# Two-level gates of two blocks from the fifth group on, with attention's turns copied by ScalarE and the leftovers' norm in three parts

## The chip, the cores and the metric

The kernel runs on one core of a Trainium2 chip. Its time is the device time of one execution, in microseconds (us). A profile of one execution is read beside it. The engines are named as the profile names them: PE (TensorE, with PEld for its weight loads), DVE (VectorE), ACT (ScalarE), POOL (GpSimd) and SP (SyncE, which here only issues DMAs).

## What is computed

An attention block without softmax is followed by a multiplicative feed-forward block. All arithmetic is in float32.

```python
# q, k, v: (8 batches, 8 heads, 576 tokens, 64)
kv  = einsum('bhsd,bhse->bhde', k, v)
o   = einsum('bhsd,bhde->bhse', q, kv)
x   = o / sqrt(mean(o*o, axis=-1, keepdims=True) + 1e-06) * g_norm
x   = x.transpose(0, 2, 1, 3).reshape(8 * 576, 512)
out = ((x @ w1) * (x @ w2)) @ w3 @ w_out   # w1, w2: 512x1024; w3: 1024x1024; w_out: 1024x512
```

## The kernel before

**Groups.** The 4608 tokens are worked on in nine groups of 512: groups 0 to 6 are the first 512 tokens of batches 0 to 6, then comes group 8, the 64 leftover tokens of all eight batches, and group 7 (batch 7) is last. The kernel counts them by T in the order 0, 1, ..., 6, 8, 7. w3 @ w_out is folded into one matrix (w3o) at the start. A group has two parts: the *gates*, which make a = x @ w1, b = x @ w2 and their product, and the *projection* of the product with w3o.

**One-level gates.** The 1024 columns of the gates are cut into four pairs of blocks, p = 0 to 3. `gates(T, p, ...)` computes one pair by Winograd's form of Strassen's scheme (`winograd`): seven products instead of eight, each of two weight matrices by two chunks of 128, so 28 matmuls of 128x128 weights by 256 moving columns. Sums of weights (s1 to s4) are kept in SBUF; sums of the inputs (t1 to t4) are made once a group by `combine_x`, in the projection before. After a product ScalarE copies it out of PSUM (`keep`), because the next product is added on top of it in the same bank, or VectorE adds two and multiplies the a half by the b half (`multiply`: L784, L785).

**Two-level gates.** For the last two groups, T = 8 and 7 (`TWICE`), blocks p = 0 and 1 are done together with the scheme applied twice (`gates_of_two`): seven products for each of the two weight matrices (w), each of seven matmuls of 128x128 by 128 columns, 98 in all. The second-level sums of the weights are made by `prepare_w` in seven steps during groups 3 and 4, stored in DRAM (`w_l2`), and loaded as three parts into the three buffers called `streams`, which the projection uses too. `replace_a21` overwrites the weights' a21 quarters with the fourth sum, in group 6. The second-level sums of the inputs are 28 subtractions of 128x128 on GpSimd (`sum_x`, L844 to L847). ScalarE copies accumulators (L888, L889), VectorE adds others to them in halves (`add`, L893 and L894), and `finish` makes four quarters of the result from seven places of an accumulator (L905 to L908), with the gate product (L910) for the second w. The order of such a group is: gates of p = 2, two-level gates of p = 0 and 1, gates of p = 3, projection. The projection (`project_twice`) is two-level in every group from 1 on; its first matmuls read the gate product c11 of the block p = 3 and the inner sums made from it (`sum_inner`).

**Attention for the next group.** `steps(b)` hands out pieces of the attention of batch b, where b = T + 1. `between()` runs one piece at two places of each one-level block, eight a group:

- `begin_kv`: PE's kv products (L339) of two pairs of heads, copied by ScalarE (L350).
- `finish(h)`: PE's products q by kv (L415) of half h, and `norm`: ScalarE squares (L383), VectorE sums (L384), ScalarE takes the root (L388), VectorE inverts (L390) and multiplies into `xn` (L393).
- `q_two_by_dma`, `x_by_dma`: a transpose of 512 columns through DMA. Before it, GpSimd copies the tile into two planes of 16 bits (L296, L298); SP issues the transpose (L300); after it, GpSimd copies the planes back together (L310). `turn(i, ...)` begins one in piece i and ends it one piece later.
- In odd batches, `product_left` (L434) with its norm, for the leftover queries of two batches, and `x_left_by_dma`.

**Order.** PE, GpSimd and SP run in the order in which the code is written. VectorE does so from block p = 3 to the end of a projection, and in `gates_of_two`; elsewhere VectorE and ScalarE are ordered by a scheduler, with `tc.issue_after(x)` placing an instruction behind x on its engine. PSUM has eight banks: five in the pool `ps_mm` (gates and projection), three in `ps_at` (attention, and the accumulator r3 of the two-level gates).

Of the kernel before, what the change touches and what calls it, by code (L numbers as in the profile page):

```python
# [22 lines left out]
def kernel(  # L23
# [40 lines left out]
    KF = DF // P  # L64
    NH = KF // 2
# [254 lines left out]
    def attention(b):  # L320
# [41 lines left out]
        def q_by_dma(r):  # L362

            qT[r] = work.tile([P, 2, 2, P], FP32, name="qT")
            q_sb = loaded["q", b, r].rearrange("p e n -> p (e n)")
            to = qT[r].rearrange("p e i t -> p (e i t)")
            return turn_by_dma([q_sb], to, q_sb, [to], q_copy)
# [3 lines left out]
        def q_left_by_dma():  # L371
# [3 lines left out]
            return turn_by_dma([src], to, src, [to], q_copy)  # L375

        def norm(o_ps, dsts):

            n, w = len(o_ps), o_ps[0].shape[1]
            inv = work.tile([P, n, w // D], FP32, name="inv")  # L380
            for i in range(n):
                sq = work.tile([P, G], FP32, name="sq")[:, 0:w]
                nc.scalar.activation(sq, o_ps[i], AF.Square)  # L383
                nc.vector.tensor_reduce(  # L384
                    out=inv[:, i], in_=sq.rearrange("p (h d) -> p h d", d=D), axis=AX.X, op=ALU.add
# [39 lines left out]
        def product_left():  # L425
# [16 lines left out]
            all_of(norm(o_ps, [xn[:, :, e:e + 1, :] for e in range(2)]))  # L442
# [10 lines left out]
        def x_by_dma(h, copy=nc.gpsimd.tensor_copy):  # L453
# [4 lines left out]
            half = [slice(r * G, (r + 1) * G) for r in range(2)]  # L458
            return together(
                turn_by_dma(  # L460
                    [xn[:, :, r * P:(r + 1) * P]], flat[:, half[r]], turned[:, half[r]], [x[:, :, r]],
                    copy,
                )
                for r in range(2)
            )

# [37 lines left out]
        def finish(h):  # L504
# [4 lines left out]
            q_two_by_dma, q_left_by_dma, x_by_dma, x_left_by_dma,  # L509
        )})  # L510

    batches = {}

    def batch(b):
        if b not in batches:
            batches[b] = attention(b)
        return batches[b]

    def steps(b):
# [25 lines left out]
        odd = b % 2  # L545
        if b == 1:
# [12 lines left out]
        if b == 1:  # L559
# [19 lines left out]
            ends[5].append((end, "left", "u3"))  # L579
        else:  # L580
# [8 lines left out]
        if odd:  # L589
            fs[second].append((a.product_left,))  # L590
# [3 lines left out]
        else:  # L594
            turn(5, a.x_by_dma, 1)
            if odd:
                turn(5, a.x_left_by_dma, next_group=more)
        if more:
            turn(7 if b == 1 else 5, batch(b + 1).q_two_by_dma, 0, 1, next_group=True)
# [39 lines left out]
    def winograd(lhsT, rhs, chunks, done, between=lambda: None, keep_u3=True):  # L639
# [17 lines left out]
        def keep(name, ps):  # L657
            t = late_tile(name)[:, 0:4, :].rearrange("p (u a) n -> p u (a n)", u=2)
            copies.setdefault(name, []).append(nc.scalar.copy(t, ps))  # L659
            late[name] = t  # L660
# [109 lines left out]
    def gates(T, p, between, ready=lambda name: None):  # L770
# [4 lines left out]
        def multiply(name, one, two):  # L775

            dst = ab[int(name[1]) - 1][:, p, int(name[2]) - 1, :]
            if two is None:
                c = late_pool.tile([P, N], FP32, name="c21")
                nc.scalar.copy(c, one[:, 0, :])  # L780
# [15 lines left out]

    def prepare_w():
# [631 lines left out]
```

## Time and profile before

| what | us |
|---|---|
| median of 3 runs | 759.11 (758.6 to 759.81) |
| the profiled execution | 758.72 |
| its span, first to last instruction | 756.9 |
| PE busy in the span | 749.4 |
| DVE busy | 589.4 |
| ACT busy | 267.0 |
| POOL busy | 164.1 |
| group T = 5 (467.08 to 542.52 of the span) | 75.44 |
| group T = 8 (617.26 to 685.20) | 67.94 |

The granted clock of TensorE is 1.00 throughout. A profile line of a group of instructions gives line, engine, operation, the tiles as out<-in, shapes, how many, then busy time and the mean of one in ns, then how long the engine had been idle before them and what ended that. In the chain of waits each line gives start, length, and what ran; weight loads are counted together with matmuls there.

### The profile page before, as it was taken

To read this page: it belongs to the slowest core of one execution; us is meant where nothing else is said; L and a number is where in the kernel's file an instruction comes from. 1 tells how busy PE (TensorE), PEld (TensorE's weight loads), DVE (VectorE), ACT (ScalarE), POOL (GpSimd) and SP (SyncE) were. 2 spreads that over 40 slices of the span, in tenths; PEclk is the share of its full clock that TensorE was granted. 3 is DMA by queue.
4 is the path that set the end of the run, shared out by engine and by line. 5 is a ranking of instruction groups with operands and counts; after the bars stand their busy time and mean duration, and the time that the engine had idled before them with its cause. 6 is when DMAs were issued, how large, how long until landed. Compare 5 with 4: busy or idle time off the path is not lost.

```text
span 756.9 us, 14948 instructions
## 1 busy us (share of the span) xinstructions
PE 749.4 (99%) x5903; PEld 657.7 (87%) x5903; DVE 589.4 (78%) x1171; ACT 267.0 (35%) x492; POOL 164.1 (22%) x190
## 2 busy tenths in 40 slices
PE   8999999999999999999999999999999999999998
PEld 5455788888899889988998899889988999999997
DVE  7977999639888568758975897567776778996897
ACT  6777787312322232223222322232223223222321
POOL 0000000322511441144114410431143124006000
PEclk9999999999999999999999999999999999999999
DMA  9996954349997845675767567745743470465244
GB/s 319 344 334 177 273 163 102 85 104 271 336 299 248 225 114 177 223 205 141 218 218 210 155 192 223 208 103 173 224 125 53 150 225 28 146 211 186 87 152 139
DMA packets 146554, 143.20 MB, mean 189 GB/s; under 512 B 86580, under 2 KB 133812, under 8 KB 146484
## 3 DMA queue, kind: packets, MB, share of 16 engines
q1 hardware_dynamic: 144032, 127.82, 58.1%
q10 hardware_dynamic: 2452, 14.42, 5.7%
q8 instruction: 47, 0.77, 0.4%
q14 instruction: 23, 0.19, 0.1%
HBM read 105.78 MB, written 19.14 MB: 165 GB/s over the span
## 4 chain that ended last, share of the span: by engine, by line
PE 97%; DVE 1%; DMA 1%; ACT 1%; issue 0%; SPq 0%; ACTq 0%
PE mm L646 55%; PE mm L1075 23%; PE mm L625 7%; PE mm L875 5%; PE at L339 3%; PE at L415 2%; PE at L612 1%; PE at L875 1%; DMA raw<-in_moe_w_out_dram 1%; PE at L1126 0%; DVE ab L163 0%; PE at L358 0%; PE at L434 0%; DVE chunks L170 0%; SPq L198 0%
## 5 line engine op out<-in xcount | busy, mean ns | idle before, releaser
L646 PE MATMUL mm<-xT,w_sb 128*128 128x256 f32 x720 | 165.2, 380 | 0.0
L646 PEld LDWEIGHTS mm<-xT,w_sb 128*128 128x128 f32 x720 | 136.6, 191 | 18.3 <-issue 0.5
L646 PE MATMUL mm<-xc,ws 128*128 128x256 f32 x512 | 116.2, 380 | 0.0
L646 PEld LDWEIGHTS mm<-xc,ws 128*128 128x128 f32 x512 | 97.3, 190 | 13.7 <-ACT p L659 0.8
L296 POOL COPY xT<-xn 128x1024 uint16<-128x1024 uint16 x26 | 31.2, 1227 | 171.9 <-DVE xn L393 171.9
L784 DVE TENSOR_TENSOR c<-mm,u 128x512 f32<-128x512 f32 x32 | 22.0, 689 | 58.4 <-PE mm L646 58.4
L659 ACT COPY u<-mm 128x512 f32<-128x512 f32 x58 | 34.0, 585 | 93.4 <-PE mm L646 82.8
L659 ACT COPY p<-mm 128x512 f32<-128x512 f32 x66 | 38.7, 586 | 73.9 <-PE mm L646 68.5
L646 PE MATMUL mm<-xc,w_sb 128*128 128x256 f32 x256 | 61.4, 383 | 0.0
L625 PE MATMUL mm<-chunks,ab 128*128 128x512 f32 x128 | 60.1, 603 | 1.0 <-DVE chunks L173 1.0
L646 PE MATMUL mm<-xT,ws 128*128 128x256 f32 x240 | 57.4, 383 | 0.0
L785 DVE TENSOR_TENSOR ab<-c 128x256 f32<-128x256 f32 x96 | 53.8, 561 | 2.5
L646 PEld LDWEIGHTS mm<-xc,w_sb 128*128 128x128 f32 x256 | 48.0, 190 | 6.9 <-ACT u L659 0.3
L646 PEld LDWEIGHTS mm<-xT,ws 128*128 128x128 f32 x240 | 45.1, 190 | 6.2
L1075 PE MATMUL mm<-w3o_sb,ab 128*128 128x128 f32 x368 | 48.7, 276 | 0.0
L1075 PE MATMUL mm<-w3o_sb,raw 128*128 128x128 f32 x372 | 48.1, 276 | 0.0
L384 DVE TENSOR_REDUCE inv<-sq 128x8 f32<-128x512 f32 (+1 forms) x40 | 23.4, 627 | 30.0 <-ACT sq L383 30.0
L1075 PEld LDWEIGHTS mm<-w3o_sb,ab 128*128 128x128 f32 x368 | 45.4, 192 | 0.5
L780 ACT COPY c<-mm 128x256 f32<-128x256 f32 x32 | 11.9, 372 | 95.4 <-PE mm L646 95.4
L1075 PEld LDWEIGHTS mm<-w3o_sb,raw 128*128 128x128 f32 x372 | 44.8, 192 | 0.0
L1086 ACT COPY u<-mm 128x512 f32<-128x512 f32 x23 | 13.5, 586 | 85.3 <-DVE raw L1099 46.6
L310 POOL COPY xT<-xn 128x1024 uint16<-128x1024 uint16 x26 | 31.6, 1244 | 54.0 <-DMA xn<-xT 54.0
(300 smaller groups left out, 1378.7 us busy)
## 6 DMA issues: line engine op xcount, KB each, us to landing
w3o_sb<-w3o_l SPq DMA_DIRECT2D x18, 896.0 KB, 5.4
raw<-in_moe_w_dram SPq DMA_DIRECT2D x31, 512.0 KB, 7.1
raw<-w3o_l SPq DMA_DIRECT2D x15, 896.0 KB, 4.7
w3o_sb<-w3o_l ACTq DMA_DIRECT2D x14, 896.0 KB, 4.6
k_sb<-in_k_dram SPq DMA_DIRECT2D x32, 256.0 KB, 4.5
v_sb<-in_v_dram SPq DMA_DIRECT2D x32, 256.0 KB, 4.7
q_sb<-in_q_dram SPq DMA_DIRECT2D x32, 256.0 KB, 3.3
out_dram<-raw SPq DMA_DIRECT2D x14, 512.0 KB, 4.3
```

Source lines behind the costliest of these rows:

```text
L296: copy(to, src.rearrange("p a n w -> p w a n"))
L310: copy(words(dst), src)
L339: nc.tensor.matmul(kv_ps[e * D:(e + 1) * D, r - rs[0], :], lhsT=k_sb[:, e, cols] if j < J else kl[:, 2 * r + e, :], rhs=v_sb[:, e, cols] i ...
L384: nc.vector.tensor_reduce(out=inv[:, i], in_=sq.rearrange("p (h d) -> p h d", d=D), axis=AX.X, op=ALU.add)
L415: nc.tensor.matmul(o_ps[l][tokens, n * D:(n + 1) * D], lhsT=qT[r][rows, e, i, tokens], rhs=kv_b[rows, e, r, :], start=True, stop=True,)
L625: nc.tensor.matmul(sums_ps[half][m], lhsT=w3T[half, c][:, m, :], rhs=chunks[:, c, 1, :], start=(c == 0), stop=(c == KF - 1),)
L646: nc.tensor.matmul(ps[:, u, :], lhsT=lhsT(a_name, u, c), rhs=rhs(b_name, c),  start=(u == 0 and c == 0 and to is None), stop=(c == chunks ...
L659: copies.setdefault(name, []).append(nc.scalar.copy(t, ps))
L784: adds.setdefault(name, []).append(nc.vector.tensor_add(c, one, two))
L785: nc.vector.tensor_mul(dst, c[:, 0, :], c[:, 1, :])
L875: nc.tensor.matmul(ps[place // 4][:, place % 4, :], lhsT=x, rhs=y, start=new and place // 4 not in seen, stop=True, skip_group_check=True,)
L1075: nc.tensor.matmul(to[:, i, :], lhsT=x[:, c, :], rhs=y[:, c, :], start=new and place // 4 not in seen, stop=(c == 1), skip_group_check=True,)
```

## The change

The tuple `IN_TWO` takes the place of `TWICE` for most decisions: groups 4, 5 and 6 now also run blocks p = 0 and 1 as two-level gates, between p = 2 and p = 3. These three groups carry attention work (batches 5, 6 and 7), the last two do not. With that:

- `sum_x` becomes eight subtractions on VectorE, of 128x512 and 128x384, at the start of the group. Its results lie where the one-level weight sums of p = 0 and 1 were.
- Those weight sums are therefore stored in DRAM as well. `w_l2` holds 66 blocks in five parts in place of three; the loads are spread over the two-level gates, and the first three parts of the projection are loaded at their end.
- The weights' sums are made in groups 2 and 3, `replace_a21` runs in group 3.
- For batches 5 to 7 the copies before and after the turns of q and x are ScalarE's, each placed behind a named accumulator copy (`turns_by_scalar`, `run_slot`). The leftovers' x is still turned with GpSimd.
- For batches 5 and 7 `product_left` moves to piece 6, in block p = 3, and its norm is cut in three: squares at once, sums and root after c12, the rest after c22.
- The two-level gates use the five banks of `ps_mm` alone. In groups 4 to 6 VectorE's order inside them is the scheduler's.

The diff, cut to its core:

```diff
+    FIRST_OF_TWO = 4
...
-        def norm(o_ps, dsts):
+        def norm(o_ps, dsts, squares_first=False):
             n, w = len(o_ps), o_ps[0].shape[1]
             inv = work.tile([P, n, w // D], FP32, name="inv")
+            sq = []
+            def square(i):
+                if squares_first and i:
+                    sq.append(sq[0][:, w:2 * w])
+                else:
+                    at = 0 if b > FIRST_OF_TWO else i
+                    sq.append(work.tile([P, G], FP32, name=f"sq{at}", bufs=1))
+                nc.scalar.activation(sq[i][:, 0:w], o_ps[i], AF.Square)
+            if squares_first:
+                for i in range(n):
+                    square(i)
+                yield
             for i in range(n):
-                sq = work.tile([P, G], FP32, name="sq")[:, 0:w]
-                nc.scalar.activation(sq, o_ps[i], AF.Square)
+                if not squares_first:
+                    square(i)
                 nc.vector.tensor_reduce(
...
-            all_of(norm(o_ps, [xn[:, :, e:e + 1, :] for e in range(2)]))
+            dsts = [xn[:, :, e:e + 1, :] for e in range(2)]
+            if b <= FIRST_OF_TWO:
+                all_of(norm(o_ps, dsts))
+            else:
+                left_norm.append(norm(o_ps, dsts, True))
+                next(left_norm[0])
...
+        def x_part_by_dma(h, r, copy):
...
+    slots, stage = {}, [None]
+    def run_slot(key, behind):
+        for f, *args in slots.pop(key, []):
+            with tc.issue_after(behind.ins):
+                f(*args)
...
+    def turns_by_scalar(b):
+        a, turning = batch(b), {}
+        def at(key, *call):
+            slots.setdefault(key, []).append(call)
+        def begin(name, f, *args):
+            turning[name] = f(*args, nc.scalar.copy)
+            next(turning[name])
+            if name[0] == "q":
+                next(turning[name])
+            elif name[2]:
+                for r in range(2):
+                    next(turning["x", name[1], r])
...
+        for r in (2, 3):
+            at((0, 0), begin, ("q", b, r), a.q_by_dma, r)
+        if b % 2:
+            at(("p2", "c21"), begin, ("q", "left"), a.q_left_by_dma)
+            at((0, 3), end, ("q", "left"))
+        at((0, 6), end, ("q", b, 2))
+        at((1, 0), end, ("q", b, 3))
+        for h, begins, ends in (
+            (0, ((0, 3), (0, 3)), ((1, 3), (1, 3))),
+            (1, (("p3", "p1"), ("p3", "p5")), (("p3", "c21"), ("proj", "p1"))),
+        ):
+            for r in range(2):
+                at(begins[r], begin, ("x", h, r), a.x_part_by_dma, h, r)
+                at(ends[r], end, ("x", h, r))
+        if b + 1 < B:
+            n = batch(b + 1)
+            for r in range(2):
+                at(("p3", "u2"), begin, ("q", b + 1, r), n.q_by_dma, r)
+                at(("proj", ("u2", "u3")[r]), end, ("q", b + 1, r))
...
+            turns_by_scalar(b)
...
-            fs[second].append((a.product_left,))
+            fs[6 if by_scalar else second].append((a.product_left,))
...
+    PRODUCTS = [
+        ("a11", "b11"), ("a12", "b21"), ("s2", "t2"), ("s1", "t1"), ("s3", "t3"), ("s4", "b22"),
+        ("a22", "t4"),
+    ]
+    BLOCKS = {}
+    for w in range(2):
+        for n, (name, _) in enumerate(PRODUCTS):
+            keys = ("a11", "a12", "a22", "s3") if name in ("s1", "s2", "s4") else ()
+            for key in (*keys, "s1", "s2", "s4"):
+                BLOCKS[w, n, key] = len(BLOCKS)
+    IN_PART = PART // P
+    W_PARTS = -(-len(BLOCKS) // IN_PART)
...
+            blocks = {"s1": s1, "s2": s2, "s4": s4, "a11": a11, "a12": a12, "a22": a22}
+            for key, t in blocks.items():
+                if (0, n, key) in BLOCKS:
+                    store_w(n, key, t)
...
+            if (0, n, "s3") in BLOCKS:
+                store_w(n, "s3", a21)
...
+            of_xc, of_xT = (free["w", p] for p in range(2))
+            of_xc, of_xT = (t.rearrange("p s w c m -> p (s w c m)") for t in (of_xc, of_xT))
+            x_sums.append([
+                *(of_xT[:, i * 4 * P:(i + 1) * 4 * P].rearrange("p (n t) -> p n t", t=P) for i in range(3)),
+                work.tile([P, G], FP32, name="sq1", bufs=1).rearrange("p (n t) -> p n t", t=P),
+            ])
+            x_sums.append([
+                of_xc[:, i * 3 * P:(i + 1) * 3 * P].rearrange("p (n t) -> p n t", t=P) for i in range(4)
+            ])
+        whole = xT[T].rearrange("p i j c n -> p (i j) c n"), xc
+        for (t1, t2, t4, t3), x in zip(x_sums, whole):
+            b11, b12, b21, b22 = (x[:, :, c, i * P:(i + 1) * P] for c in range(2) for i in range(2))
+            nc.vector.tensor_sub(t1, b12, b11)
+            nc.vector.tensor_sub(t2, b22, t1)
+            nc.vector.tensor_sub(t3, b22, b12)
+            nc.vector.tensor_sub(t4, b21, t2)
...
+        mm = [bank(ps_mm, "mm").rearrange("p (i n) -> p i n", n=P) for _ in range(5)]
+        plan = [((0, 1), (2, 3), (4, 2)), ((3, 4), (2, 0), (1, 2))]
+        names = [("p1", "p5", "u2", "p1"), ("u2", "p5", "p1", "u2")]
...
+            load(w, n)
+            if n in (2, 5):
+                between()
             return ps
-        def banks(pool, tag):
-            return [bank(pool, tag).rearrange("p (i n) -> p i n", n=P) for _ in range(2)]
-        def keep(t, ps):
+        def load(w, n):
+            last = max(at for (v, m, _), at in BLOCKS.items() if (v, m) <= (w, n))
+            if last + 1 >= (len(loaded_w) - len(streams) + 1) * IN_PART:
+                load_w()
+            if (w, n) == (1, len(PRODUCTS) - 1):
+                for _ in range(3):
+                    load_b()
+        def keep(name, ps, at):
+            t = late_tile(name)
             nc.scalar.copy(t[:, 0:4], ps[0])
-            nc.scalar.copy(t[:, 4:7], ps[1][:, 0:3])
+            run_slot(at, nc.scalar.copy(t[:, 4:7], ps[1][:, 0:3]))
...
+            r1, r3, r2 = ([mm[i] for i in pair] for pair in plan[w])
+            of_p1, of_u2, of_p5, of_last = names[w]
+            products(0, w, r1, True)
+            p1 = keep(of_p1, r1, (w, 0))
+            products(1, w, r3, True)
             add(p1, r3)
             finish(p1, w, 0, 0)
             products(2, w, r1, False)
-            z = keep(late_tile("u2"), r1)
-            r2 = products(3, w, banks(ps_mm, "mm"), True)
-            p5 = keep(places[1] if w else late_tile("p5"), r2)
+            z = keep(of_u2, r1, (w, 2))
+            products(3, w, r2, True)
+            p5 = keep(of_p5, r2, (w, 3))
...
+    IN_TWO = (*range(FIRST_OF_TWO, B - 1), *TWICE)
...
-            if T == B - 2 and p == 2 and not replaced:
+            if T == FIRST_OF_TWO - 1 and p == 2 and not replaced:
                 replaced.append(True)
                 replace_a21()
-        if T in TWICE:
-            once = iter([T])
-            gates(T, 2, lambda: [sum_x(t) for t in islice(once, 1)])
-            run(sum_ab(2))
-            in_order = tc.manual_schedule(engines={mybir.EngineType.DVE})
-            in_order.__enter__()
-            gates_of_two(T)
+        if T in IN_TWO:
+            p = 2
+            stage[0] = "p2"
+            with tc.issue_after(adds["out"].ins):
+                sum_x(T)
+            gates(T, p, between)
+            run(sum_ab(p))
+            if T in TWICE:
+                in_order = tc.manual_schedule(engines={mybir.EngineType.DVE})
+                in_order.__enter__()
+            gates_of_two(T, between)
             of_two = sum_ab_two()
             for _ in range(2):
                 of_two.pop(0)()
         for p in range(NF):
-            if T in TWICE and p + 1 < NF:
+            if T in IN_TWO and p + 1 < NF:
                 continue
+            stage[0] = f"p{p}" if T in IN_TWO else None
             if T and p + 1 == NF:
                 sum_1, sum_2, sum_4, sum_3 = sum_ab(p)
                 following = {
                     "c21": [sum_4],
                 }
-                if T in TWICE:
-                    following["c12"] += of_two[:1]
-                    following["c22"] += of_two[1:]
-                else:
+                if T in IN_TWO:
+                    following["c12"] += [lambda: all_of(next(t) for t in left_norm for _ in range(2)), *of_two[:1]]
+                    following["c22"] += [lambda: all_of(left_norm.pop()) if left_norm else None, *of_two[1:]]
+                if T not in TWICE:
                     in_order = tc.manual_schedule(engines={mybir.EngineType.DVE})
                     in_order.__enter__()
...
-                    for _ in range({(3, 1): 2, (3, 2): 2, (4, 1): 2, (4, 2): 1}.get((T, p), 0)):
+                    for _ in range({(2, 0): 1, (2, 1): 1, (2, 2): 1, (3, 0): 2, (3, 1): 2}.get((T, p), 0)):
```

## The prediction

> **What bounds the kernel now.** I read the page first, then the chain of waits in order of time, then the table of stretches, one group at a time, then VectorE's timeline where the two-level form already runs. The page:
>
> ```profile
> PE 749.4 (99%) x5903; PEld 657.7 (87%) x5903; DVE 589.4 (78%) x1171; ACT 267.0 (35%) x492; POOL 164.1 (22%) x190
> PE 97%; DVE 1%; DMA 1%; ACT 1%; issue 0%; SPq 0%; ACTq 0%
> ```
>
> TensorE (PE) is 97% of the chain that ended last. So a shorter stream of matmuls shortens the kernel, as long as nothing makes PE wait. The chain by time, sixth group (T=5) and then the leftovers' group (T=8); the counts include weight loads, so x56 is 28 matmuls:
>
> ```profile
> 467.08 10.36 PE mm L646 x48
> 477.44 1.32 PE at L339 x40
> 478.76 1.09 PE at L415 x64
> 479.85 19.19 PE mm L646 x88
> ...
> 501.45 19.19 PE mm L646 x88
> 520.64 21.88 PE mm L1075 x196
> ...
> 617.26 12.09 PE mm L646 x56
> 629.35 1.56 PE mm L875 x14
> 630.91 1.56 PE at L875 x14
> 632.47 9.38 PE mm L875 x84
> 641.85 1.56 PE at L875 x14
> 643.41 7.82 PE mm L875 x70
> 651.23 12.09 PE mm L646 x56
> 663.32 21.89 PE mm L1075 x196
> ```
>
> Four one-level gate blocks cost 10.36 + 19.19 + 19.19 = 48.74 us. With two of them in the two-level form they cost 12.09 + 21.88 + 12.09 = 46.06. No gap follows either. The table of stretches, same two groups (columns: length, then busy time of PE, PEld, DVE, ACT, POOL, then the granted clock, DMA share, GB/s):
>
> ```profile
> 467.08:542.52 75.44, 75.44 (x630) 68.93 (x629) 50.97 (x108) 20.27 (x43) 19.75 (x19) 1.00 0.60 175
> 617.26:685.20 67.94, 67.94 (x505) 65.10 (x505) 57.34 (x127) 18.57 (x35) 13.69 (x29) 1.00 0.46 152
> ```
>
> The two-level group carries no attention work and still needs 57.34 us of VectorE (DVE) in 67.94. VectorE's timeline at its last block shows how little is left (the bracket is idle time before the instruction):
>
> ```profile
> 647.54 0.69 DVE L893 TENSOR_TENSOR xT<-mm,xT 128x512 f32<-128x512 f32 x1 [0.66 <-PE mm L875]
> 655.94 0.69 DVE L910 TENSOR_TENSOR ab<-ab,c 128x512 f32<-128x512 f32 x1
> 658.25 0.69 DVE L784 TENSOR_TENSOR c<-mm,u 128x512 f32<-128x512 f32 x1 [0.28 <-PE mm L646]
> 662.04 0.68 DVE L784 TENSOR_TENSOR c<-mm,p 128x512 f32<-128x512 f32 x1
> 662.75 0.42 DVE L785 TENSOR_TENSOR ab<-c 128x256 f32<-128x256 f32 x1
> ```
>
> The last line is the gate product c11 of block p3. It ends at 663.17, and the projection, whose first matmuls read it, starts at 663.32: slack 0.15 us. PE has no slack to give after a two-level stage, and the change puts attention work into three such groups.
>
> **TensorE's part.** Groups 4, 5 and 6 each change two one-level blocks for one two-level stage: 48.74 - 46.06 = 2.68 us less, 8.04 in all. kv (1.32), product (1.09) and leftover products (0.70, read at 425.31 to 426.01) only move.
>
> Here a rule speaks against the change. The Trainium skill, TensorE: Matmul & The Clock Gate, section Back-to-back issue gap, gives a sustained spacing of about 81 ns for 128 moving columns and 131 for 512, as each matmul also brings a weight load. On a straight line that is 98 ns at 256 (my estimate), so a half-width matmul would cost 0.83 of a full one, and 98 of them 1.45 times the 56 they replace: 11 us more per group, 33 in all. The trace has 21.88/98 = 223 ns against 19.19/44 = 436 ns, a ratio of 0.51, with weight loads of 192 ns beneath. I take the trace; the other end falls away because this very stream has run.
>
> **VectorE's part, per group.** Out go six c additions (0.69), six gate products (0.42), two c21 products (0.41) and two sets of block sums (0.43 + 3 x 0.42): 11 us. In come six accumulator additions in halves (0.69 + 0.55), eight finishes (0.29 + 3 x 0.42 = 1.55), four gate products (0.69), four sums of 128x512 (0.69): 25.4 us; and sum_x, which moves from GpSimd: four subtractions of 128x512 and four of 128x384, 5.0 us.
>
> GpSimd's 16 copies of turned q and x go to ScalarE. The row for L785 is 0.55 us mean in group 5 and 0.42 where GpSimd is idle (one at 508.76 took 1.25 beside a GpSimd copy). With the same excess in L784 (0.90 against 0.69) and L699 (0.60 against 0.42) that is 12 x 0.13 + 3 x 0.21 + 4 x 0.18 = 2.9 us back. The Trainium skill, SBUF — State Buffer, section SBUF: two separate sides, says the loser of the shared port pair (a VectorE instruction with two SBUF inputs against a GpSimd one that reads SBUF) is blocked for the whole instruction; 16 copies of 1.15 us would then hide 18 us of blocking. I take the 2.9 measured.
>
> So 50.97 - 11 + 25.4 + 5.0 - 2.9 = 67.5 us of VectorE in 72.8 of PE; groups 4 and 6 add 1.84 for the leftovers' norm (0.41 x 2, 0.19, 0.41 x 2; group 4 had it before). It fits on average, so place decides.
>
> **Where VectorE is late.** I walk the queue of the changed kernel's built order for group 5, with t = 0 at the first two-level matmul and the intervals of the leftovers' group above.
> - Start of the group: VectorE is still finishing the last projection until 2.6 us in, then sum_x to 7.6; c12 was due at 7.0. Before, VectorE idled 4.4 us here waiting for that product (474.10), so this is absorbed: cost 0, up to 0.6 if not.
> - First half: same work as at 629 to 640, where it waited 1.61. Norm of the first product ends near t = 3; the bank it delays is needed at 5.6. Cost 0.
> - Second half: after product 2 PE runs kv and product, 2.40 us. VectorE's norm for it is 0.68 x 2 + 0.25 + 0.68 x 2 = 2.97. The product ends at 18.03; ScalarE's kv copies run to 18.05, its first square to 18.7, so the first reduction ends at 19.4. In ScalarE's order the second square then stands behind the copy of p1, due at 19.0; it ends at 20.2, and the second reduction starts there: VectorE idles 0.8. The last gate product ends 7.3 us after the stage instead of 5.4 (656.63 - 651.23).
> - Block p3: its ScalarE copies p1, p5, u2 wait for tiles that VectorE is still finishing: free at 26.6, 28.6, 30.3 against needs of PE at 27.8, 29.5, 31.3, less 0.6 for the copy. All met, by 0.3 to 0.6. Then c11 starts 1.29 us after its product instead of 0.34; with 0.15 of slack PE waits 0.75 at the projection. That is new.
> - Groups 4 and 6: the left norm's three parts stand between c12, c22 and c11: 1.84 more of VectorE for 0.70 more of PE. PE waits 0.75 + 1.14 = 1.9 in group 4, where two q copies of 1.06 stand ahead of the squares, and about 0.3 less in group 6, which has none.
>
> Sum of waits: 4.25. Behind c11 in VectorE's queue stand the inner sums that the next projection products wait for; they slip together with PE and cost nothing more.
>
> **ScalarE and queues.** 16 copies of 1.04 to 1.16 us are added: 20.3 + 17.7 + about 3 = 41 of 73 us. They stand behind PE's copies at places where the next is due later: after copy 0 two q copies end at 4.3, the next copy is ready at 4.1 and needed at 6.25. Each copy back waits in ScalarE's queue for a transpose that SP issued; landing 2.9 us median (7.5 longest) against 8 us or more of distance. Cost 0 if that holds. Weights: 33 stores of 128 KB for 21, and five loads of 896 KB a group where three were, in five groups instead of two. Each lands in about 5 us; parts four and five are asked for 11 us before use, and the three projection loads at the stage's end have 12 us for the first. They pass transposes in SP's queue at 0.34 us each. Cost 0; if bandwidth fails, 1 to 2 us.
> Groups 2 and 3 take the weights' sums (1.25 a step) and replace_a21 (3.8, from group 6): group 3 rises from 58.6 to 62.4 busy, as group 1 has now (62.3) with PE full. Groups 8 and 7 get sum_x on VectorE, in the idle time named above: 0.
>
> **The sum.** 758.72 (this profiled execution: 756.9 span and 1.8 around it) - 8.04 + 4.25 = 754.93. The median of runs is 0.39 higher, so 755.3.
>
> **Rivals.**
> - VectorE keeps up: the built order interleaves finishes, saving the 0.04 us between dependent instructions, and no wait is left. Then 759.11 - 8.04 = 751.1. For it: the ledger misses by only 0.75 in group 5. Against: 0.15 us of slack before attention was added.
> - Slower: head-of-line blocking by the second norm. Its multiplications write xn, whose earlier half ScalarE must first have copied out; I have ScalarE done at 23.4 and VectorE there at 23.5, no margin at all. If that copy is late, every accumulator addition and finish behind it in VectorE's queue is late, and PE pays one for one at p3 and the projection. With waits above 2.68 a group the gain is gone; at 3.7, by 2.3 us late in all three groups, it is 762.
> - The same, less late (waits of 2.2 to 3.2 a group): 757.6 to 760.6, no change.
>
> **Chances.** About 0.2% (1.5 us) is what this kernel's measurement can tell from nothing. Forecast 0.53, keeping up 0.23, less late 0.14, slower 0.10. Range 750.8 to 758.8: from the keeping-up case to waits averaging 2.6 a group. Faster 0.76, same 0.14, slower 0.10.
>
> **What would show it.** Right: the two-level matmuls (L974 of the changed kernel) in five groups, 21.9 us plus 2.4 of attention; PE's busy share below 99% with gaps between p3's last product and the projection, 0.5 to 1 us in group 5, longer in 4 and 6, released by VectorE. GpSimd almost idle from group 4 on. Wrong: gaps inside the two-level stage released by ScalarE, or by DMA; gaps in groups 2 and 3; the norm's multiplication (L408) waiting for ScalarE.

## The result: 756.5 us against 759.0, and the profile after

| what | before | after |
|---|---|---|
| median of 6 runs each, same chip (us) | 758.95 (758.41 to 759.83) | 756.49 (755.72 to 757.2) |
| span of the profiled execution (us) | 756.9 | 754.9 |

The ratio is 0.9966, 95% interval 0.9953 to 0.9979: faster by 2.5 us, where 3.8 were forecast (755.3). Run again later beside other kernels, the changed kernel gave 756.64 against 758.78, a ratio of 0.9970 (0.9958 to 0.9982).

The page of the changed kernel, the rows for busy time and for the shares of the chain:

```profile
PE 744.5 (99%) x6155; PEld 659.2 (87%) x6155; DVE 635.8 (84%) x1301; ACT 322.4 (43%) x558; POOL 85.2 (11%) x83
PE 91%; DVE 5%; DMA 2%; ACT 1%; issue 0%; SPq 0%; DVEq 0%; ACTq 0%
```

PE is busy for 4.9 us less than before, but its part of the chain has gone from 97% to 91%. The other engines hold it up more, VectorE above all: 5% after 1%. The chain in order of time says where. It goes through the sixth group (T=5) and then the projection's start in T=6. L720 is the one-level gates, L974 the two-level ones, L1183 the projection:

```profile
467.91 10.36 PE mm L720 x48
478.27 1.32 PE at L340 x40
479.59 1.09 PE at L430 x64
480.68 1.92 PE mm L720 x8
482.61 15.63 PE mm L974 x140
...
500.64 6.45 PE mm L974 x56
507.09 12.09 PE mm L720 x56
519.18 21.88 PE mm L1183 x196
...
590.89 0.76 DVE xn_left L408 x2
...
592.89 0.55 DVE ab L861
...
595.48 0.35 DVE ab L1145
595.87 19.47 PE mm L1183 x172
```

Group 5 is PE from end to end: no wait is left in it. In group 6 the chain crosses to VectorE in block p3, passes the left norm's multiplications (L408) and the gate product c11 (L861), and comes back to PE only in the projection, which takes 21.88 us where nothing interrupts it. Group 4 looks like group 6.

From one group's first matmul to the next one's, in us:

| group | before | after | difference | predicted |
|---|---|---|---|---|
| 1 | 79.02 | 79.40 | +0.38 | 0 |
| 2 | 76.50 | 76.73 | +0.23 | 0 |
| 3 | 75.44 | 76.07 | +0.63 | 0 |
| 4 | 76.26 | 75.52 | -0.74 | -0.78 |
| 5 | 75.44 | 73.15 | -2.29 | -1.93 |
| 6 | 74.73 | 74.27 | -0.46 | -1.08 |
| 8 | 67.95 | 67.95 | 0.00 | 0 |

With what lies before group 1 (+0.33) and group 7 (-0.09) the differences add up to -2.0, the difference of the spans. The three changed groups brought 3.49 us; 0.86 was lost in groups 2 and 3, which the sum had at nothing. Group 1 runs with its DMA engines full (share 0.99). It took 78.9 to 79.6 us in those kernels that do the same work there (78.89 when the changed kernel ran again), so its 0.38 is read as scatter.

The table of stretches of groups 4, 5 and 6 (length, then busy time of PE, PEld, DVE, ACT, POOL, granted clock, DMA share, GB/s):

```profile
392.23:467.75 75.52, 74.51 (x747) 70.16 (x745) 67.48 (x150) 41.50 (x70) 4.59 (x4) 1.00 0.83 231
467.75:540.90 73.15, 73.15 (x714) 69.59 (x713) 65.12 (x147) 38.92 (x65) 2.55 (x3) 1.00 0.80 241
540.90:615.17 74.27, 73.19 (x706) 68.91 (x705) 65.89 (x149) 36.55 (x62) 2.90 (x3) 1.00 0.67 202
```

VectorE has 65 to 67 us of work in 73 to 75, ScalarE 37 to 42, and GpSimd is almost idle.

### The profile page after: what moved, and what is told of

It is laid out like the page before. It is cut to its first block, busy times and chain, and to the rows that moved or that the text cites. A ratio compares the mean times of both kernels' runs of the same rounds, so it can differ in the third digit from the quotient of the medians.

```text
span 754.9 us, 15615 instructions
## 1 busy us (share of the span) xinstructions
PE 744.5 (99%) x6155; PEld 659.2 (87%) x6155; DVE 635.8 (84%) x1301; ACT 322.4 (43%) x558; POOL 85.2 (11%) x83
## 4 chain that ended last, share of the span: by engine, by line
PE 91%; DVE 5%; DMA 2%; ACT 1%; issue 0%; SPq 0%; DVEq 0%; ACTq 0%
PE mm L720 42%; PE mm L1183 21%; PE mm L974 15%; PE mm L699 7%; PE at L340 2%; PE at L430 2%; DMA raw<-in_moe_w_out_dram 1%; DVE c L860 1%; PE at L686 1%; DMA raw<-w3o_l 1%; DVE ab L861 1%; DMA raw<-in_moe_w_dram 1%; PE at L1234 0%; DVE inv L399 0%; DVE raw L896 0%
## 5 line engine op out<-in xcount | busy, mean ns | idle before, releaser
L720 PE MATMUL mm<-xT,w_sb 128*128 128x256 f32 x576 | 132.2, 379 | 0.0
L720 PEld LDWEIGHTS mm<-xT,w_sb 128*128 128x128 f32 x576 | 108.7, 190 | 14.8 <-issue 0.5
L720 PE MATMUL mm<-xc,ws 128*128 128x256 f32 x416 | 94.8, 380 | 0.6 <-ACT p L733 0.6
L720 PEld LDWEIGHTS mm<-xc,ws 128*128 128x128 f32 x416 | 78.8, 190 | 12.4 <-ACT p L733 1.8
L733 ACT COPY u<-mm 128x512 f32<-128x512 f32 x46 | 27.0, 587 | 74.3 <-PE mm L720 59.6
L733 ACT COPY p<-mm 128x512 f32<-128x512 f32 x54 | 31.5, 586 | 51.5 <-PE mm L720 45.4
L1183 PE MATMUL mm<-w3o_sb,ab 128*128 128x128 f32 x368 | 49.3, 276 | 2.1 <-DVE ab L861 1.9
L720 PE MATMUL mm<-xc,w_sb 128*128 128x256 f32 x208 | 50.0, 383 | 0.0
L1183 PEld LDWEIGHTS mm<-w3o_sb,ab 128*128 128x128 f32 x368 | 45.5, 192 | 3.3 <-DVE ab L861 2.3
L1183 PE MATMUL mm<-w3o_sb,raw 128*128 128x128 f32 x372 | 48.1, 275 | 0.0
L720 PE MATMUL mm<-xT,ws 128*128 128x256 f32 x192 | 46.0, 382 | 0.0
L1183 PEld LDWEIGHTS mm<-w3o_sb,raw 128*128 128x128 f32 x372 | 44.8, 192 | 0.0
L399 DVE TENSOR_REDUCE inv<-sq 128x8 f32<-128x512 f32 (+1 forms) x40 | 23.9, 627 | 24.5 <-ACT sq L390 24.5
L720 PEld LDWEIGHTS mm<-xc,w_sb 128*128 128x128 f32 x208 | 38.8, 190 | 5.6
L861 DVE TENSOR_TENSOR ab<-c 128x256 f32<-128x256 f32 x78 | 41.3, 529 | 2.1
L699 PEld LDWEIGHTS mm<-chunks,ab 128*128 128x128 f32 x128 | 21.8, 190 | 23.6 <-issue 15.3
L720 PEld LDWEIGHTS mm<-xT,ws 128*128 128x128 f32 x192 | 36.0, 190 | 5.1
L974 PE MATMUL mm<-ws,w3o_sb 128*128 128x128 f32 x250 | 38.5, 275 | 0.0
L297 POOL COPY xT<-xn 128x1024 uint16<-128x1024 uint16 x14 | 17.3, 1264 | 152.4 <-DVE xn L408 152.4
```

Source lines behind the costliest of these rows:

```text
L297: copy(to, src.rearrange("p a n w -> p w a n"))
L399: nc.vector.tensor_reduce(out=inv[:, i], in_=sq[i][:, 0:w].rearrange("p (h d) -> p h d", d=D), axis=AX.X, op=ALU.add)
L699: nc.tensor.matmul(sums_ps[half][m], lhsT=w3T[half, c][:, m, :], rhs=chunks[:, c, 1, :], start=(c == 0), stop=(c == KF - 1),)
L720: nc.tensor.matmul(ps[:, u, :], lhsT=lhsT(a_name, u, c), rhs=rhs(b_name, c),  start=(u == 0 and c == 0 and to is None), stop=(c == chunks ...
L861: nc.vector.tensor_mul(dst, c[:, 0, :], c[:, 1, :])
L974: nc.tensor.matmul(ps[place // 4][:, place % 4, :], lhsT=x, rhs=y, start=new and place // 4 not in seen, stop=True, skip_group_check=True,)
```

## The experiments

Lines are quoted as those of the changed kernel; in two kernels added code moves the gates to L734 and the projection to L1197. Kernels with one place of work moved are compared by group length, since a part of a microsecond shows there.

**1. Groups 2 and 3: where the weights' sums stand.** The chain of the changed kernel in group 3:

```profile
329.08 1.18 DVE raw L896
330.26 1.18 DVE w3o_sb L896
...
332.77 1.20 DVE inv L399 x2
334.00 0.31 ACT inv L403
334.31 0.48 ACT p L733
334.83 14.08 PE mm L720 x64
```

Two steps of the weights' sums (L896 to L898) stand in VectorE's queue ahead of the norm's reductions (L399). ScalarE's root (L403) waits for those. Behind the root in ScalarE's queue stands a copy out of PSUM (L733), and PE waits for that copy. So VectorE work that no one needs soon delays PE through two queues. The edit moves the steps to blocks where VectorE is through with them before the next norm comes (in group 3 the last step then ends at 348.6, and the next reduction starts at 350.2):

```diff
-{(2, 0): 1, (2, 1): 1, (2, 2): 1, (3, 0): 2, (3, 1): 2}
+{(2, 1): 2, (2, 2): 2, (3, 1): 3}
```

> The changed kernel with the seven steps of the weights' sums moved away from the ends of block p = 0: none in (2, 0) and (3, 0), two in (2, 1), two in (2, 2), three in (3, 1). In the changed kernel groups 2 and 3 are 76.73 and 76.07 us long, against 76.50 and 75.44 before. Theory A: the steps at the end of block p = 0 stand in VectorE's queue ahead of the norm's two reductions, ScalarE's root waits for these and the copy p1 of the next block stands behind the root; with the steps elsewhere group 3 is back at 75.5 (0.6 less), group 2 at 76.4 to 76.5, and the median falls by 0.6 to 0.9 to about 755.7. Theory B: the two groups are longer by chance or by the extra stores on the DMA queues; then they stay at 76.7 and 76.1, or the loss moves to the blocks where the steps now are, and the median stays at 756.5.

Measured: 755.52 us against 758.92, ratio 0.9958 (0.9941 to 0.9974). Groups 2 and 3 take 76.26 and 75.45. Its table of stretches for group 3:

```profile
314.99:390.44 75.45, 75.45 (x631) 68.83 (x630) 59.02 (x124) 20.29 (x43) 20.21 (x19) 1.00 0.72 202
```

PE is busy for all of it, with VectorE at 59.02. Theory A holds. This kernel and the changed kernel had not been timed beside each other, so both were run side by side on one chip:

> The changed kernel with only the weights' sums at other places (2,1: two; 2,2: two; 3,1: three), run beside the changed kernel on the same chip. By the group lengths of the traces it is 0.5 us shorter in group 2 and 0.6 in group 3, so 1.0 to 1.2 us below the changed kernel: 755.4 against 756.5. If the difference of the earlier runs was chance of the chip or of transfers in group 1, the two agree within 0.3 us.

> The changed kernel itself, unedited, as the measure for the three beside it on the same chip: 756.0 to 757.0.

Measured: 755.28 (755.02 to 755.47) with the sums moved, 756.64 (755.97 to 756.97) without, five runs each, and the two do not overlap. They are 1.36 us apart, a little more than expected; in their profiled executions groups 2 and 3 make 0.96 of it, and the rest is not placed. This version beats both kernels: ratio to before 0.9952 (0.9940 to 0.9964).

**2. The waits of groups 4 and 6: the left norm.** In after, VectorE's timeline in group 6 (bracket: idle before):

```profile
586.75 0.69 DVE L860 TENSOR_TENSOR c<-mm,u 128x512 f32<-128x512 f32 x1 [0.99 <-PE mm L720]
587.48 0.43 DVE L861 TENSOR_TENSOR ab<-c 128x256 f32<-128x256 f32 x1
587.82 0.74 DVE L399 TENSOR_REDUCE inv<-sq 128x4 f32<-128x256 f32 x2
...
590.60 0.20 DVE L405 RECIPROCAL inv<-inv 128x8 f32<-128x8 f32 x1
590.89 0.42 DVE L408 TENSOR_TENSOR xn_left<-at,inv 128x256 f32<-128x256 f32 x1
591.24 0.42 DVE L408 TENSOR_TENSOR xn_left<-mm,inv 128x256 f32<-128x256 f32 x1
```

Before c12 (586.75) VectorE idles 0.99 us: it has caught up. It falls behind only between there and c11, and the left norm lies in just that stretch. First try: put it behind c11 and two of the inner sums.

```diff
-following["c12"] += [lambda: all_of(next(t) for t in left_norm for _ in range(2)), *of_two[:1]]
-following["c22"] += [lambda: all_of(left_norm.pop()) if left_norm else None, *of_two[1:]]
+following["c12"] += of_two[:1]
+following["c22"] += of_two[1:]
+following["c11"] += [lambda: all_of(left_norm.pop()) if left_norm else None]
...
-        for f in ahead:
-            f()
+        if T != B - 2:
+            for f in ahead:
+                f()
...
+            if T == B - 2:
+                for f in ahead:
+                    f()
```

> The changed kernel with all of VectorE's part of the leftovers' norm (two reductions, reciprocal, two multiplications, 1.84 us) moved behind the gate product c11 of p3 and the first two sets of inner sums, in groups 4 and 6; in group 6 the input sums for the leftovers' group are made later in the projection, so that they do not wait for the leftovers' turn. Theory A, place: what groups 4 and 6 lose (75.52 and 74.27 us long, where group 5 without that norm is 73.16) is the wait of the projection for c11; group 4 falls to 73.8 to 74.3, group 6 to 72.4 to 73.0, the median by 2.4 to 3.2 to about 753.7. Theory B, capacity: VectorE has 69.5 us of work in these groups and the same 1.84 makes PE wait inside the projection; then both groups lose less than 0.5 us and the median stays within 1 us of 756.5.

Measured: 771.66 us, ratio 1.0161 (1.0144 to 1.0178); groups 4 and 6 take 82.41 and 80.42. Neither theory had this. SP's queue in group 6:

```profile
606.94 1.58 SPq L301 DMA_TRANSPOSE xn_left<-qT_left  x1
608.57 0.99 SPq L1125 DMA_DIRECT2D xT<-w3o_l  x1
```

The transpose of the leftovers' x waits for a GpSimd copy, which waits for the late norm. Behind it in SP's queue stands the load of the projection's fourth part of weights (L1125), which needs nothing of it. PE's timeline in group 6 shows the wait for the norm and the wait for that load:

```profile
605.77 0.68 PE L1183 MATMUL mm<-raw,w3o_sb 128*128 128x128 f32 x4 [1.22 <-DVE xn_left L408]
614.05 4.18 PE L1183 MATMUL mm<-xT,raw 128*128 128x128 f32 x18 [3.57 <-DMA xT<-w3o_l]
```

Second try: the same late norm, with the transpose begun behind the loads, and the sums of the weights as in experiment 1.

```diff
-turn(7 if by_scalar else 5, a.x_left_by_dma, next_group=more or by_scalar)
...
+slots.setdefault(("proj", "u2"), []).append((begin_left,))
+if more:
+    to_end.append((end_left,))
+else:
+    slots.setdefault(("proj", "u3"), []).append((end_left,))
```

> The left norm's VectorE part goes behind c11 and the first two inner sums, as in the miss before (771.7), but the leftovers' x is turned only after the projection's part loads have been asked for (begun at the projection's u2, ended later), so no transpose stands ahead of a load in SP's queue. The weights' sums lie as in the run with only these moved (2,1: two; 2,2: two; 3,1: three), so groups 1 to 3 must stay at about 78.9, 76.3 and 75.5. Theory A (the waits of 1.55 and 1.61 us at the projection of groups 4 and 6 are the left norm standing ahead of c11, a matter of place): both go, group 4 about 74.0 and group 6 about 72.7 us, total about 3.1 below the run with only the weights' sums moved, 752.4. Theory B (VectorE has no room at all in these groups): the 1.84 us come back in the projection or at the next group's start, total 755 to 756. Theory C (another queue is late next: SP, or the turned leftovers): a gap with a DMA or GpSimd as its releaser in the projection, total above 757.

Measured: 756.73 us, ratio 0.9974 (0.9965 to 0.9982), slower than experiment 1's kernel without it (0.9952). The load wait is gone, and theory A's gain did not come. PE's timeline in group 6:

```profile
597.09 0.68 PE L1197 MATMUL mm<-raw,w3o_sb 128*128 128x128 f32 x4 [1.23 <-DVE xn_left L408]
```

One of the leftover products lies in a bank of the pool that the projection uses (xn_left<-mm above). Until the norm has read it, the projection's next product has no bank. The projection takes 23.27 and 23.35 us in groups 4 and 6, where 23.43 and 23.49 were measured with the norm ahead of c11. The late `combine_x` costs group 8 another 1.07 us. The wait only changed its place. Theory B had said so (755 to 756; measured 0.7 more), but for another reason: it is the bank that PE is seen to wait for. Whether VectorE would have held PE all the same is open, since a bank of its own for the leftover product was not tried.

**3. Is it ScalarE's copies that make the change pay?** The turns' copies of groups 4 to 6 go back to GpSimd:

```diff
-turning[name] = f(*args, nc.scalar.copy)
+turning[name] = f(*args, nc.gpsimd.tensor_copy)
```

> The changed kernel with the copies before and after the turns of q and x in groups 4 to 6 back on GpSimd (16 a group) and ScalarE without them. Theory A: beside GpSimd's copies VectorE's additions and products of two SBUF inputs take longer, about 2.9 us a group as in group 5 before the change; VectorE has no room for that after the two-level stage, so groups 4 to 6 grow by 1 to 3 us each and the median goes to 759 to 765, no better than before the change. Theory B: VectorE's idle time in these groups (7 to 10 us each) takes it up; groups 4 to 6 grow by less than 0.5 us each and the median stays below 758. Theory C: ScalarE's copies are what delays PE's accumulator copies; then the groups get shorter.

Measured: 773.67 us, ratio 1.0198 (1.0181 to 1.0214). Groups 4, 5 and 6 take 85.04, 77.91 and 79.59, which is 9.5, 4.8 and 5.3 more: theory A's direction at more than its size (1 to 3 a group). VectorE's busy time there is 79.34, 73.06 and 73.17, which is 7.3 to 11.9 us more for the same instructions. The groups by shape show which: the halves of `add` (L999), the 128x128 additions of `finish` and its 128x256 ones, first in the changed kernel, then with GpSimd copying (busy us, mean ns; two of the five groups that these rows cover are the same in both):

```profile
L999 DVE TENSOR_TENSOR p<-mm,p 128x512 f32<-128x512 f32 x20 | 13.7, 686 | 3.5 <-PE mm L974 3.5
L1011 DVE TENSOR_TENSOR p<-p 128x128 f32<-128x128 f32 x25 | 7.1, 284 | 0.4
L1013 DVE TENSOR_TENSOR ab<-p 128x256 f32<-128x256 f32 x15 | 6.4, 424 | 0.4
```

```profile
L999 DVE TENSOR_TENSOR p<-mm,p 128x512 f32<-128x512 f32 x20 | 13.7, 684 | 3.5 <-PE mm L974 3.5
L1011 DVE TENSOR_TENSOR p<-p 128x128 f32<-128x128 f32 x25 | 11.9, 477 | 0.4
L1013 DVE TENSOR_TENSOR ab<-p 128x256 f32<-128x256 f32 x15 | 9.7, 646 | 0.4
```

The first line of each fence is the control: additions with one operand in PSUM keep their time (686 and 684 ns). Only those with both operands in SBUF are stretched. A rival would be that GpSimd's copies come too late for PE. The list of PE's waits speaks against it: apart from one at the program's start it names VectorE and ScalarE alone. The largest is that for c11 (us in all, times, longest):

```profile
PE mm L1183 <- DVE ab L861: 4.0, 3, 2.1
```

**4. How much room has VectorE at a group's start?** `sum_x` is done twice, 5.0 us more of VectorE:

```diff
 with tc.issue_after(adds["out"].ins):
     sum_x(T)
+    sum_x(T)
```

> The changed kernel with the eight subtractions of sum_x made twice in a row at the start of groups 4, 5, 6, 8 and 7 (5.0 us more of VectorE each; the values are the same). Theory A: one sum_x just fills the idle time that VectorE has at the start of a group (it ends 7.6 us in, c12 is due at 7.0); a second one makes c12 5.6 us late, the copy u3 waits for c12's tile and PE for u3, so each of the five groups grows by 2 to 4 us and the median goes to 766 to 774. Theory B: block p2 has more room than its first wait shows; the groups grow by less than 1 us each and the median stays below 761.

Measured: 773.8 us, ratio 1.0194 (1.0172 to 1.0216). Group 4 lengthens by 3.5, 5 by 2.0, 6 by 1.7, 8 by 5.2 us. PE's timeline in group 4:

```profile
406.01 1.99 PE L720 MATMUL mm<-xc,w_sb 128*128 128x256 f32 x8 [1.63 <-ACT u L733]
412.63 0.71 PE L974 MATMUL mm<-xc,w3o_sb 128*128 128x128 f32 x4 [1.50 <-ACT p L994]
```

Theory A holds, with group 6 a little under its 2 to 4 us and group 8 over: one `sum_x` fills the idle time at the start, and a second reaches PE by way of ScalarE's copies.

**5. Do the changed groups hand lateness on?** Group 4 stays one-level:

```diff
-    FIRST_OF_TWO = 4
+    FIRST_OF_TWO = 5
```

> FIRST_OF_TWO is 5 in place of 4, so group 4 stays one-level and only groups 5 and 6 change form; the left norm of batch 5 runs whole in group 4. Theory A (each changed group brings 2.68 us of PE less its own waits, independent of the others): group 4 goes back to 76.3 us, up to 0.6 more because the overwriting of a21 now lies there; groups 5 and 6 stay at 73.15 and 74.27; total 0.7 to 1.3 above the changed kernel, 757.2 to 757.8. Theory B (the three groups hand lateness on to each other, VectorE starting each behind): groups 5 and 6 get shorter by over 0.3 us when 4 is one-level, total at or below the changed kernel's 756.5.

Measured: 757.07 us, ratio 0.9982 (0.9975 to 0.9989); group 4 takes 76.26, groups 5 and 6 take 73.16 and 74.26. They do not notice what group 4 does, so each group's gain stands by itself: theory A. Group 4 is as long as in the kernel before, though it overwrites a21 in place of three steps of the weights' sums. The total is a little under the 757.2 to 757.8 expected.

**6. One group more.** FIRST_OF_TWO = 3 on top of the kernel with the late norm, the weights' sums in groups 1 and 2 ({(1, 1): 1, (1, 2): 2, (2, 1): 4}):

> FIRST_OF_TWO is 3: group 3 is two-level too, on top of the kernel with the late left norm and late turn; the weights' sums move to groups 1 and 2 (1,1: one; 1,2: two; 2,1: four). Group 3 carries attention of batch 4, an even batch, so no leftovers: it should look like group 5. Theory A (PE's saving of 2.68 with no wait, as measured in group 5): group 3 from 75.45 to about 73.15, that is 2.3 us below the late-norm kernel, less up to 1 us for the weights' sums in groups 1 and 2: 750 to 751.5. Theory B (the weights' sums are the expensive part: seven steps of about 1.25 us of VectorE plus the overwriting of a21 in two groups that are full): groups 1 and 2 lengthen by 2 us or more together and the total stays within 1 us of the late-norm kernel.

Measured: 764.7 us, ratio 1.0079 (1.0058 to 1.0100). Group 3 did what group 5 had done: 73.26 us, 2.19 less. But group 1 took 89.1. Its table of stretches (the window starts 0.4 us early), and two of VectorE's waits in it:

```profile
159.77:249.27 89.50, 82.40 (x648) 74.61 (x646) 64.21 (x138) 20.39 (x43) 20.05 (x19) 0.96 0.95 270
```

```profile
224.91 0.42 DVE L1155 TENSOR_TENSOR w3o_sb<-raw 128x256 f32<-128x256 f32 x1 [3.41 <-DMA w_l<-w3o_sb]
229.35 0.43 DVE L1156 TENSOR_TENSOR w3o_sb<-w3o_sb,raw 128x256 f32<-128x256 f32 x1 [4.02 <-DMA w_l<-w3o_sb]
```

VectorE is hardly busier (64.21 us) than in the changed kernel, where group 1 needs 79.40 with 63.03. SP's queue in that group shows why:

```profile
211.46 8.40 SPq L301 DMA_TRANSPOSE xn<-xT  x2
219.95 2.61 SPq L301 DMA_TRANSPOSE q_sb<-qT  x2
222.65 1.04 SPq L903 DMA_DIRECT2D w_l<-w3o_sb  x2
```

The stores of the weights' sums (L903) stand behind four transposes that take 11 us to issue. VectorE must not overwrite w3o_sb until the store has read it, and PE waits for these inner sums (L1155, L1156), 1.3 and 3.8 us. Another 2.0 us of waiting in this group begins with a weights' step that itself waits 3.1 us for an earlier DMA, and PE's busy time is 3 us longer at the lower granted clock. So the sums were tried in group 2 alone, where the DMA share is 0.76, once at two places and once at one (left norm as in the changed kernel):

```diff
-    FIRST_OF_TWO = 4
+    FIRST_OF_TWO = 3
-{(2, 0): 1, (2, 1): 1, (2, 2): 1, (3, 0): 2, (3, 1): 2}
+{(2, 0): 3, (2, 1): 4}
```

> FIRST_OF_TWO is 3, the left norm as in the changed kernel, and all seven steps of the weights' sums go to group 2 (2,0: three; 2,1: four), none to group 1, whose DMA share was 1.00 and which lost 10.6 us when three steps were put there. Group 3 should be 73.2 to 73.3 us, as measured with group 1 loaded (73.26), against 75.45. Theory A (the cost was group 1's full DMA queues, not VectorE): group 2 has a DMA share of 0.76 with four steps, takes three more and lengthens by 0 to 1 us, group 1 stays at 78.9: total 1.2 to 2.2 below the kernel with only the weights' sums moved, 753.3 to 754.5. Theory B (VectorE's queue is the cost: 61.9 us busy in group 2 with four steps, plus 3.9 for three more and 3.8 for overwriting a21, is 69.6 in 76.3): group 2 lengthens by 2 us or more, total 756 or above.

> As the split kernel, but all seven steps stand at one place of group 2 (2,1: seven). The seven steps are 8.75 us of VectorE in one piece. Theory A (place decides: a piece of VectorE work ahead of a norm delays ScalarE's root and the copies behind it): group 2 lengthens more than in the split kernel, by 2 to 5 us. Theory B (only the sum over the group matters): same length as in the split kernel within 0.3 us.

Measured: 756.32 us, ratio 0.9966 (0.9955 to 0.9978), with the steps at two places; 761.21, ratio 1.0030 (1.0018 to 1.0042), with all seven at one. Group 3 takes 73.26 and 73.15, group 2 takes 78.47 and 85.53, against 76.39 in the run beside them with four steps there. PE's longest wait in group 2, first with two places, then with one:

```profile
259.26 1.99 PE L720 MATMUL mm<-xc,ws 128*128 128x256 f32 x8 [1.53 <-ACT p L733]
```

```profile
285.90 3.78 PE L720 MATMUL mm<-xc,w_sb 128*128 128x256 f32 x8 [6.56 <-ACT u L733]
```

With two places it is the wait of group 3 above, larger: a norm behind the sums, ScalarE's root and copy behind the norm. With one place the norms stand behind the sums too, but the last link differs. ScalarE is through with its root and waits for a tile that VectorE's next gate addition (L860) must free, and that addition stands behind sums and norms in VectorE's own queue:

```profile
285.26 0.58 ACT L733 COPY u<-mm 128x512 f32<-128x512 f32 x1 [2.61 <-DVE c L860]
```

Place decides: the second run's theory A, though with 7.1 us more where 2 to 5 were expected. For the first run theory A was too hopeful, and theory B's lengthening came (2.1 us), but 1.5 of it is one wait behind one norm, not a lack of room. What group 3 gains, group 2 loses, so experiment 1's kernel stays the best.

## Why the prediction was right, and where it was not

- **TensorE's saving: 2.68 us a group predicted, 2.29 measured.** The step was mis-sized, and the chain shows why. An uninterrupted block takes 12.09 us and an uninterrupted two-level stage 21.88. Cut by attention products they take 10.36 + 1.92 = 12.28 and 15.63 + 6.45 = 22.08. Each cut costs 0.2. The 48.74 of the one-level form had its cuts in it; the 46.06 came from the leftovers' group, which has none. Twice 0.2 is the missing 0.39.
- **Half-width matmuls at 0.51 of a full one**, the trace against the rule that the prediction quotes: upheld. No group shows the 11 us that the rule would have cost.
- **Group 5's wait of 0.75: not there.** The last gate product ends 6.23 us after the stage instead of 7.3 (513.32 against 507.09), and VectorE still idles 0.17 us before c12. The term that failed is the price of VectorE's new work. It was taken from the leftovers' group, where VectorE does one addition or finish after the other: two additions, three finishes and three gate products fill 9.09 us there (647.54 to 656.63 in the kernel before). In group 5 the scheduler interleaves them. The same work, with 2.0 us of the norm and of a block sum in its midst, fills 9.79 us (503.53 to 513.32), so 7.8 without them. An instruction that needs the result of the one ahead starts 0.03 to 0.04 us after its end, one that doesn't starts some 0.08 us before it. Over the whole group the 25.4 us come to 22.1 of VectorE's time, by the starts and ends in the trace. That is the reason given for the rival "VectorE keeps up": in this group the rival was right.
- **2.9 us back when GpSimd stops copying: held.** In group 5 of the kernel before, GpSimd's copies stretched four VectorE instructions with both inputs in SBUF (at 491.07, 506.53, 508.76 and 510.05), by 2.9 us in all. In the changed kernel two subtractions of sum_x lose 0.9 of it again to copies that GpSimd still makes. With the 16 copies back on GpSimd (experiment 3) 15 instructions are stretched there, and VectorE is busy 7.9 us longer.
- **The rule on the shared port pair** (the Trainium skill, SBUF — State Buffer, section SBUF: two separate sides) stood at 18 us and was set aside for 2.9. The trace of the kernel before has the 2.9, and experiment 3 has 7.3 to 11.9. A single meeting does look as the page says: GpSimd's two copies of 1.19 us at 328.78 in group 3 lie over the two L896 that took 1.26 and 1.25 us on VectorE, whose neighbours took 0.41. What the 18 us leave out is that many copies meet no such instruction: in group 5 of the kernel before 5 of GpSimd's 19 did.
- **Waits of 1.9 and 1.6 in groups 4 and 6: 1.55 and 1.61** (projection 23.43 and 23.49 less 21.88). The sizes are near, but of two terms both were off. The 0.75 inherited from group 5 is 0: VectorE idles 0.99 us before c12 in both groups. The left norm's own 1.14 was too small. From the start of c12 to that of c11 VectorE takes 4.52 us in group 5 (514.09 to 518.61), 6.06 in group 4 and 6.14 in group 6 (586.75 to 592.89). The 1.54 and 1.62 more are PE's wait. The prediction had set PE's 0.70 us for the leftover products against the norm; but these products run ahead of c12, where VectorE idles anyway.
- **Groups 2 and 3 at cost 0: failed**, 0.23 and 0.63. The prediction added busy time (62.4 us in group 3, as group 1) and did not walk VectorE's queue there, as it had for group 5, though it names gaps in these groups as a sign of being wrong. VectorE is busy for only 60.39 us in group 3; the delay comes from the place of the steps in its queue. Experiment 1 takes both back.
- **sum_x absorbed, ScalarE's copies, DMA at 0: held.** ScalarE is 38.92 us busy in group 5 (41 predicted). c12 starts 8.19 us into group 5 (475.94), later than the 7.0 at which it was due, and PE still does not wait. In the second half VectorE idles 0.92 us for the second square (0.8 predicted). The rival of head-of-line blocking did not occur, but only just: ScalarE's copy out of xn ends at 505.58, and VectorE's multiplications into xn (L408) start at 505.61. The prediction had named this as having no margin:

```profile
502.93 0.69 DVE L399 TENSOR_REDUCE inv<-sq 128x8 f32<-128x512 f32 x1 [0.92 <-ACT sq L390]
503.53 0.68 DVE L999 TENSOR_TENSOR p<-mm,p 128x512 f32<-128x512 f32 x1
...
504.42 1.16 ACT L311 COPY xT<-xn 128x1024 uint16<-128x1024 uint16 x1
...
505.61 1.29 DVE L408 TENSOR_TENSOR xn<-at,inv 128x512 f32<-128x512 f32 x2
...
512.63 0.69 DVE L1016 TENSOR_TENSOR ab<-ab,c 128x512 f32<-128x512 f32 x1
...
514.09 0.69 DVE L860 TENSOR_TENSOR c<-mm,u 128x512 f32<-128x512 f32 x1 [0.17 <-PE mm L720]
...
518.61 0.42 DVE L861 TENSOR_TENSOR ab<-c 128x256 f32<-128x256 f32 x1
```

So the forecast of the three changed groups (-3.79) met the measured -3.49 through errors that nearly cancel, which is luck. The saving was 1.0 us too large in all (0.39, 0.39 and, since group 6 had been 0.14 longer than group 5 before, 0.25). The waits were 1.1 too large (4.25 against 3.16). And the leftover products cost group 6 0.36 more: before they stood right behind other products of attention (0.46 us), now they cut the gates a third time (0.82). The path was right: PE bounds the kernel, and in groups 4 and 6 it waits for c11 at the projection. What separates 755.3 from 756.5 lies mostly in groups that it had not walked.

## What to carry to other kernels

Work that nothing needs soon is only free if nothing urgent stands behind it: before putting it into an engine's idle time, walk that queue and the next engine's to the first instruction that the bounding engine waits for, and do the same for DMA queues. When a stream of matmuls is priced from another stage, take it with as many interruptions as it will have; when another engine's work is, look whether it will run in the same order. When a bounding wait is moved, ask which buffer its data holds until then; here a PSUM bank gave the wait back.

## What was not expected of the hardware

- A cut in a stream of matmuls by others of another shape costs PE 0.2 us: 12.28 and 22.08 us in groups 4, 5 and 6, where 12.09 and 21.88 are measured without one.
- SP issues in order. A transpose that is not ready (groups 4 and 6 in the first try of experiment 2) or takes long to issue (group 1 in experiment 6) holds up plain loads and stores that need nothing of it. In the first try PE waited 7.9 us in all for the two loads behind such a transpose; groups 4 and 6 were 7.0 and 6.3 us longer than in the second try, part of it at a lower granted clock.
- The granted clock fell to 0.96 in groups where PE waited for long: in groups 4 and 6 of that first try, in group 4 with GpSimd copying, in the 89.50 us row above, and in group 2 with all seven steps at one place. Whether the waits caused that is not shown.
